# One logits product of 42 columns per token tile, denominators summed by GpSimd, and batch 0's lane on three shared banks

## The chip, the core and the metric

The kernel runs on one core of a Trainium2 chip. The metric is the device time of one execution in microseconds (us), as the median of several runs. The engines are TensorE (PE in the profile, its weight loads PEld), VectorE (DVE), ScalarE (ACT), GpSimd (POOL) and SyncE (SP), which issues most of the DMAs.

## The reference

Two parts are chained. The first is an attention through 49 "agents" for four batches of 10048 tokens of 128 channels; the second sends each token to one expert of 16 (4 groups of 4), a two-layer network.

```python
a2k = softmax(scale * agents @ k.T)      # 49 x 10048 for each batch
agent_v = a2k @ v                        # 49 x 128
x = softmax(scale * q @ agents.T) @ agent_v   # 10048 x 128 for each batch
g = argmax(x @ w_group)                  # 4 groups
e = argmax(x @ w_expert[g])              # 4 experts of the group
out = p_g * p_e * (relu(x @ w1[g, e]) @ w2[g, e])
```

All inputs and outputs are float32.

## The kernel before, in words

**Tiles.** The tokens of a batch are 79 tiles of 128 (the last has 64). A chunk is 8 tiles; there are ten a batch. The attention's output x is never made for the tokens: each token keeps its 49 numerators (as a high and a low float16 part, 98 rows, transposed into a tile `et`), and the agents' values are multiplied into the expert's first matrix and into the routers' matrix. So the logits of a tile are the product of 98 rows of `et` with a small matrix `rh` of 98 x 2 x 21: 4 group logits, 16 expert logits and the numerators' sum, in a high and a low part.

**The main path.** Most tokens of a batch go to one expert, its "main" one. For each group of four tiles (`natural`, 20 a batch) the two functions `first` and `second` (lines 834 and 850) run eight units each: `first` multiplies `et` by a block of the expert's first matrix into a PSUM bank `ph` (128 x 512), ScalarE takes the ReLU as float16 (`hh`) and VectorE the remainder (`hl`); `second` comes eight units later and adds three products for each of four tiles into a bank `po`. After eight units VectorE scales `po` by the token's weight (`oo`) and SP writes it out. `ph` has three banks (pool `ps1`), `po` two (`ps2`); the other three banks (`psa`, tiles named `at`) are for everything else. Tokens of batch 0 that go to another expert are gathered and done with the last tiles of batch 3.

**Lanes.** Everything else of a batch is a lane: a Python generator that issues a few instructions and yields. Lane "a" is a batch's agents (`agents_of`, line 398): the keys' scores in `key_scores`, the maximum, and then the values. Lane "q" (`rest`, line 822) is its queries, its logits, its routing and its expert's weights. Lane "f" is batch 0's own queries, logits and routing from the second chunk on, and lane "o" prepares the left-over tokens of batch 0. A planner (`advance`, line 1144) interleaves lanes with the main path's units: each lane has a span of main path time (`SPAN_A`, `SPAN_Q`, `SPAN_F`, `SPAN_O`), the counted work of its instructions (VectorE's with weight 1, PE's and ScalarE's with 0.3), and an expected total in `WORK` (line 76); after each unit it is advanced to the part of its total that its span says. GpSimd's instructions are not counted. The first batch's start, before any main path, is written out by hand (`front`).

A lane's stages run skewed by one chunk each: for one step of the lane, the later stages of earlier chunks are issued first. For the queries the stages are the load, the split into high and low halves (ScalarE `xh`, GpSimd `xl`), the scores into a bank, the exponentials (VectorE takes the maximum `mq` and the difference `ef` out of that bank), the split of the numerators (`rows`), the transposes (two banks) and, in batch 0, the logits (one bank).

**Banks.** A lane takes its banks with `bank(b)` (line 148). For batches 1 to 3 it is always one of the three `at` banks. For batch 0 it goes round in eights:

```python
if b == 0:
    turns[0] += 1
    k = turns[0] % 8
    if k in (0, 3, 6):
        return ps1.tile([P, TS], F32, name="ph")
    if k in (1, 4):
        return ps2.tile([P, TQ, C], F32, name="po").rearrange("p a c -> p (a c)")
return psa.tile([P, 512], F32, name="at", tag="at")
```

**Logits** (`logits_of`, line 594). For each tile two matmuls of 21 columns, with the high and the low half of `rh`, add up in the same PSUM columns; ScalarE copies a chunk's 8 x 21 columns into `lg`.

**The agents' values** (`value_split`, line 352, and `value_products`, line 377; batches 1 to 3). VectorE subtracts the maximum from a chunk's scores in `S`, ScalarE takes the exponential and its float16 copy `sh`, GpSimd the remainder `sl` in pieces of three tiles (line 373). PE adds three products per tile (`vh` by `sh`, `vh` by `sl`, `vl` by `sh`) into 49 columns of one bank, `acc`, which is held for the whole stage. The denominators are summed on PE too: a matrix of ones times `sh` and times `sl`, four tiles (196 columns) at a time, into the next columns of the same bank.

The instructions that go through the counting helper carry its line, L122, in the profile; GpSimd's carry their own.

Of the kernel before, what the change touches and what calls it, by code (L numbers as in the profile page):

```python
# [10 lines left out]
F32 = mybir.dt.float32  # L11
F16 = mybir.dt.float16
I32 = mybir.dt.int32
AF = mybir.ActivationFunctionType
ALU = mybir.AluOpType
AX = mybir.AxisListType
# [4 lines left out]
P = 128  # L21
# [3 lines left out]
NA = 49  # L25
# [4 lines left out]
NT = 79  # L30
NTP = NT + 1
LAST = N - (NT - 1) * P
CT = 8
TS = 512
TQ = TS // P
# [6 lines left out]
RW = NA + 1  # L42
VS = 16.0
ES = 2.0 ** 14
ZT = 4
IC = 8
GT = 16
NGR = -(-NT // GT)
# [24 lines left out]
SPAN_O = (2.93, 3.32)  # L73
SPAN_F = (0.0, 0.52)
WA = (0.3, 1.0, 0.3)
WORK = {"a": 38e3, "q": 42e3, "o": 37.5e3, "f": 38e3}


def const_pack():
# [47 lines left out]
def build(ctx, tc, qT, kT, v, agT, wr, w1, w2, cpk, out):  # L127
    nc = tc.nc
    pool, sync = nc.gpsimd, nc.sync
    work = np.zeros(3)  # L130
    pe = Counted(nc.tensor, work, 0, 4.0, 0.42)
    vec = Counted(nc.vector, work, 1, 65.0, 1.04)
    act = Counted(nc.scalar, work, 2, 100.0, 0.83)
# [4 lines left out]
    sm = ctx.enter_context(tc.tile_pool(name="sm", bufs=2))  # L138
# [4 lines left out]
    psa = ctx.enter_context(tc.tile_pool(name="psa", bufs=3, space=PSUM))  # L143

    turns = [0]
    loaded = {}

    def bank(b=1):

        if b == 0:  # L150
            turns[0] += 1
            k = turns[0] % 8
            if k in (0, 3, 6):
# [4 lines that stand above are left out]
# [21 lines left out]
    ones16 = const.tile([P, P], F16, name="ones16")  # L179
    vec.memset(ones16, 1.0)  # L180
    ones = const.tile([P, P], F32, name="ones")
# [52 lines left out]
    def skewed(n, *stages):  # L234

        for i in range(n + len(stages) - 1):
            yield "chunk"
            for k in reversed(range(len(stages))):
                if 0 <= i - k < n:
                    yield from stages[k](i - k)  # L240
# [8 lines left out]
    def key_load(b, ci, early=None):  # L249

        st = state[b]
        if ci == 0:
            st["S"] = rt.tile([P, NT, NA], F32, name="S", tag="S")
            st["mch"] = sm.tile([P, len(chunks), NA], F32, name="mch")
            st["part"] = []
        st["k", ci] = split_load("k", b, ci, early)
        yield

    def load_only(kind, b, ci):

        if (kind, b, ci) not in loaded:
            loaded[kind, b, ci] = load(kind, b, ci)
        yield
# [88 lines left out]
    def value_split(b, ci):  # L352

        st = state[b]
        S, mb = st["S"], st["part"][0][2]
        t0, t1 = chunks[ci]
        vf = st.pop(("v", ci))
        sh, sl = [mo.tile([P, CT, NA], F16, name=name) for name in ("sh", "sl")]
        vh, vl = [wk.tile([P, CT * P], F16, name=name, tag="x" + name[1]).rearrange("p (t c) -> p t c", c=C) for name in ("vh", "vl")]
        for a, z, m in ((t0, min(t1, NT - 1), P), (NT - 1, t1, LAST)):  # L360
            if z <= a:
                continue
            x, y = S[0:m, a:z], slice(a - t0, z - t0)
            vec.tensor_sub(out=x, in0=x, in1=mb[0:m].broadcast_to([m, z - a, NA]))
            act.activation(x, x, AF.Exp, bias=shift[0:m])
            act.activation(vh[0:m, y], vf[0:m, y], AF.Copy, scale=VS)
            yield
            act.activation(sh[0:m, y], x, AF.Copy)
            vec.scalar_tensor_tensor(out=vl[0:m, y], in0=vf[0:m, y], scalar=VS, in1=vh[0:m, y], op0=ALU.mult, op1=ALU.subtract)
            for i in range(0, z - a, 3):  # L370
                j = slice(i, min(i + 3, z - a))
                w = slice(y.start + j.start, y.start + j.stop)
                pool.tensor_sub(out=sl[0:m, w], in0=x[:, j], in1=sh[0:m, w])  # L373
            yield
        st["v", ci] = sh, sl, vh, vl

    def value_products(b, ci):

        st = state[b]
        sh, sl, vh, vl = st.pop(("v", ci))  # L380
        if ci == 0:
            st["acc"] = bank(1)
        acc = st["acc"]
        t0, t1 = chunks[ci]
        for t in range(t0, t1):
            m = min(P, N - t * P)
            i = t - t0
            for x, y in (vh, sh), (vh, sl), (vl, sh):
                pe.matmul(acc[:, 0:NA], x[0:m, i], y[0:m, i], start=(t == 0 and x is vh and y is sh), stop=False)
            if i % 4 == 3 or t == NT - 1:  # L390
                yield
        for a, z, m in [(t, min(t + ZT, t1, NT - 1), P) for t in range(t0, min(t1, NT - 1), ZT)] + [(NT - 1, NT, LAST)] * (t1 == NT):
            o = acc[:, NA + (a % ZT) * NA:NA + (a % ZT + z - a) * NA]
            for y in sh, sl:
                pe.matmul(o, ones16[0:m], y[0:m, a - t0:z - t0].rearrange("p t a -> p (t a)"), start=False, stop=(z == NT and y is sl))
        yield

    def agents_of(b):

        state[b] = {}  # L400
        st = state[b]
        n = len(chunks)
        yield from skewed(n, lambda ci: load_only("k", b, ci), lambda ci: key_load(b, ci), lambda ci: key_scores(b, ci))
        yield from key_max(b, 0, n, False)
        yield from skewed(n, lambda ci: value_load(b, ci), lambda ci: value_split(b, ci), lambda ci: value_products(b, ci))
        yield
        acc = st["acc"]
        za = sm.tile([P, NA], F32, name="za2")
        vec.tensor_reduce(out=za, in_=acc[:, NA:(ZT + 1) * NA].rearrange("p (t a) -> p a t", a=NA), axis=AX.X, op=ALU.add)
        vec.tensor_scalar(out=za, in0=za, scalar1=1e-9 * ES, scalar2=None, op0=ALU.add)  # L410
        vec.reciprocal(out=za, in_=za)
        avT = sm.tile([P, NA], F32, name="avT")
        vec.scalar_tensor_tensor(out=avT, in0=acc[:, 0:NA], scalar=1.0 / VS, in1=za, op0=ALU.mult, op1=ALU.mult)
        yield
        yield from agents_scaled(b, avT)
# [106 lines left out]
    def queries_of(b, early=None, cs=None, *more):  # L522

        cs = list(range(len(chunks))) if cs is None else cs
        xs = [{} for _ in chunks]
        stages = [query_load, query_scores, query_exp, query_split, query_turn]
        if early:
            groups = [stages[:2]] + [[x] for x in stages[2:]]
        else:
            groups = [[lambda b, ci, x, early: load_only("q", b, ci)]] + [stages[:1], stages[1:2], stages[2:4], stages[4:]]  # L530

        def run(group):
            def f(i):
                for stage in group:
                    yield from stage(b, cs[i], xs[cs[i]], early)
            return f

        yield from skewed(len(cs), *[run(g) for g in groups], *[lambda i, f=f: f(b, cs[i]) for f in more])
# [53 lines left out]
    NL = NG + NE + 1  # L592

    def logits_of(b, ci):

        st = state[b]
        if ci == 0:
            st["lg"] = rt.tile([P, NL, NTP], F32, name="lg", tag="lg")
            vec.memset(st["lg"][:, :, NT:NTP], 1.0)
        lg = st["lg"]  # L600
        t0, t1 = chunks[ci]
        pl = bank(b)
        for t in range(t0, t1):
            o = pl[:, (t - t0) * NL:(t - t0 + 1) * NL]
            for h in range(2):
                pe.matmul(o, st["et", t // TQ][:, t % TQ * P:(t % TQ + 1) * P], st["rh"][:, h], start=(h == 0), stop=(h == 1))
            if t % 4 == 3:
                yield
        plv = pl[:, 0:(t1 - t0) * NL].rearrange("p (t g) -> p t g", g=NL)
        act.activation(lg[:, :, t0:t1].rearrange("p g t -> p t g"), plv, AF.Copy)  # L610
        yield

    def routing(b, t0, t1):
# [253 lines left out]
    def natural(b, w):  # L867

        t, n = TILES[w]
        return dict(b=b, w=w, t=t, n=n, per=1, units=FB, et=state[b]["et", w],  # L870
                    wb=wbuf[b % 2].bitcast(F16), done=rows_out)
# [280 lines left out]
    def lane(kind, b, gen, span):  # L1152
        lanes.append(dict(kind=kind, b=b, gen=gen, start=span[0], end=span[1], total=WORK[kind], done=0.0))

    later = queries_of(0, None, list(range(1, len(chunks))), logits_of, ranged)
    for _ in range(AHEAD):
        for x in later:
# [6 lines left out]
    for b in range(1, B):  # L1164
        lane("a", b, agents_of(b), SPAN_A[b])
        lane("q", b, rest(b), SPAN_Q[b])
# [3 lines left out]
    for b in range(B):  # L1170
# [3 lines left out]
        for w in range(NW):  # L1174
            y = next(y for y in lanes if y["kind"] == "f")
            while b == 0 and (("et", w) not in state[0] or state[0]["covered"] < TILES[w][0]):
                advance(y, y["done"] / y["total"] + 1e-6)
            x = natural(b, w)
            units = [(x, k) for k in range(FB)]
            if b == B - 1 and w >= NW - TAKEN:  # L1180
                j = w - (NW - TAKEN)
# [4 lines left out]
                y = late.pop(j)  # L1186
# [49 lines left out]
```

## Time and profile before

| | |
|---|---|
| median of three runs | 1016.2 us (1013.15 to 1016.98) |
| the profiled execution's own time | 1020.15 us |
| its span, first to last instruction | 1018.4 us |
| mean granted clock of PE | 0.974 |
| busy: PE, PEld, DVE, ACT, POOL | 946.3, 763.3, 781.8, 653.9, 331.7 us |

The profile has names of tiles on both sides of an arrow: `hl<-ph,hh` writes `hl` from `ph` and `hh`. A duration of a matmul runs from its start to the end of its results; matmuls overlap, so what one costs in a stream is the time from start to start. In the timeline, the bracket at the end of a row is the idle time ahead of it and what ended it. In a row of a group, after the bar come the busy time, the mean of one in ns, and the idle time ahead with what ended it. Pieces of a timeline that are merged have a count (x2) and one duration for all.

### The profile page before, as it was taken

The page shows a single profiled execution, that of the slowest core. Times are in us where ns is not written, and L with a number is a line of the kernel's source. Part 1 is how long each engine was busy: PE and PEld are TensorE (multiplying, and loading weights), DVE is VectorE, ACT ScalarE, POOL GpSimd, SP SyncE. Part 2 cuts the span into 40 slices and gives each one's busy share as a digit, 9 for nine tenths or more (in the row PEclk, how much of TensorE's full clock was granted, in tenths as well). Part 3 has the DMA queues.
Part 4 walks back from the last instruction along what each step waited for, and adds up shares of the span by engine and source line. Part 5 has one row for each costly group of instructions (what it writes and reads, how often), then busy time and mean ns, then how long its engine had stood idle before and what let it go on. Part 6 is the DMA issues. An engine that isn't in the chain of part 4 may idle for free. (4 is left out here: it accounts for less than half of the span.)

```text
span 1018.4 us, 32113 instructions
## 1 busy us (share of the span) xinstructions
PE 946.3 (93%) x13645; PEld 763.3 (75%) x13645; DVE 781.8 (77%) x1508; ACT 653.9 (64%) x1168; POOL 331.7 (33%) x548
## 2 busy tenths in 40 slices
PE   4968998989997999999989999999999999999996
PEld 3846777777876878888768778887777778888885
DVE  5668889977697896786977877877989966666663
ACT  4436577688745876977467778876555555555552
POOL 2334237278303624850025327630000021322211
PEclk9968999989998999999999999999999999999999
DMA  9634235444036633410463434311233062333330
GB/s 296 208 115 150 60 105 185 126 137 122 23 106 236 195 102 106 122 40 23 131 222 111 143 95 126 98 29 40 75 113 111 23 205 66 119 117 110 90 108 26
DMA packets 107451, 117.45 MB, mean 115 GB/s; under 512 B 5479, under 2 KB 92648, under 8 KB 105120
## 3 DMA queue, kind: packets, MB, share of 16 engines
q1 hardware_dynamic: 105760, 113.40, 35.8%
q0 software_dynamic: 1536, 1.90, 0.8%
q8 instruction: 108, 1.77, 0.7%
q14 instruction: 47, 0.39, 0.1%
HBM read 81.92 MB, written 33.65 MB: 113 GB/s over the span
## 5 line engine op out<-in xcount | busy, mean ns | idle before, releaser
L122 DVE SCALAR_TENSOR_TENSOR hl<-ph,hh 128x512 f16<-128x512 f32 (+1 forms) x688 | 458.7, 678 | 145.2 <-ACT hh L122 143.9
L122 PEld LDWEIGHTS <-hh 128*128 128x128 f16 x5440 | 448.1, 98 | 148.1 <-issue 4.2
L122 ACT ACTIVATE hh<-ph 128x512 f16<-128x512 f32 (+1 forms) x688 | 402.2, 591 | 220.7 <-PE ph L122 208.0
L122 PE MATMUL po<-wbuf,hh 128*128 128x128 f16 x5440 | 537.9, 220 | 0.0
L122 PE MATMUL po<-wbuf,hl 128*128 128x128 f16 x2720 | 496.0, 220 | 0.0
L122 PE MATMUL ph<-et,wbuf 98*128 98x512 f16 (+1 forms) x1280 | 384.0, 380 | 23.4 <-DVE hl L122 21.2
L122 PEld LDWEIGHTS <-hl 128*128 128x128 f16 x2720 | 266.8, 98 | 2.4 <-issue 0.6
L231 POOL TENSOR_TENSOR xl<-xf,xh 128x256 f16<-128x256 f32 (+1 forms) x288 | 189.4, 690 | 238.6 <-ACT xh L122 229.6
L122 PEld LDWEIGHTS <-wbuf 98*128 98x128 f16 x1472 | 116.8, 98 | 38.1 <-issue 30.5
L122 ACT ACTIVATE xh<-xf 128x1024 f16<-128x1024 f32 x80 | 83.3, 1041 | 53.2 <-PE at L122 27.7
L373 POOL TENSOR_TENSOR sl<-S,sh 128x147 f16<-128x147 f32 (+1 forms) x90 | 43.4, 510 | 97.0 <-ACT sh L122 93.8
L122 PEld LDWEIGHTS <-xh 128*128 128x128 f16 x1264 | 60.6, 99 | 14.6 <-ACT xh L122 12.7
L1065 POOL DMA_INDIRECT out<-oo,sidx x24 | 24.1, 1004 | 138.6 <-DVE oo L122 135.0
L1043 POOL DMA_INDIRECT er<-erow,gidx x24 | 24.7, 1030 | 134.7 <-DVE gidx L122 127.7
L574 POOL TENSOR_TENSOR rows<-ef,rows 128x147 f16<-128x147 f32 (+2 forms) x117 | 50.8, 461 | 52.3 <-ACT rows L122 52.3
L122 PEld LDWEIGHTS <-xl 128*128 128x128 f16 x632 | 53.0, 99 | 12.4 <-POOL xl L231 9.2
L122 PE MATMUL at<-agh,xl 128*128 128x49 f16 x538 | 54.1, 186 | 6.6 <-POOL xl L231 6.6
L122 DVE TENSOR_TENSOR oo<-po,cw 128x512 f32<-128x512 f32 x80 | 53.8, 673 | 6.0 <-PE po L122 5.7
L122 PE MATMUL at<-agh,xh 128*128 128x49 f16 x538 | 54.4, 187 | 3.0 <-ACT xh L122 3.0
L122 PE MATMUL at<-agl,xh 128*128 128x49 f16 x538 | 54.2, 186 | 0.0
L122 ACT ACTIVATE et<-at 98x512 f16<-98x512 f16 x68 | 39.4, 590 | 7.1 <-PE at L122 7.0
L122 DVE SCALAR_TENSOR_TENSOR vl<-vf,vh 128x1024 f16<-128x1024 f32 (+2 forms) x33 | 38.7, 1172 | 5.6 <-ACT vh L122 5.5
(278 smaller groups left out, 873.3 us busy)
## 6 DMA issues: line engine op xcount, KB each, us to landing
out<-oo SPq DMA_DIRECT2D x76, 256.0 KB, 2.7
xf<-kT SPq DMA_DIRECT2D x36, 512.0 KB, 4.1
vf<-v SPq DMA_DIRECT2D x36, 512.0 KB, 5.7
xf<-qT SPq DMA_DIRECT2D x36, 512.0 KB, 4.1
wbuf<-wall SPq DMA_DIRECT2D x12, 1024.0 KB, 4.9
erow<-rows SPq DMA_DIRECT2D x3, 1975.0 KB, 7.3
w1f<-w SPq DMA_DIRECT2D x6, 512.0 KB, 4.0
w2f<-w SPq DMA_DIRECT2D x6, 512.0 KB, 7.2
```

Source lines behind the costliest of these rows:

```text
L122: return f(*a, **k)
L231: pool.tensor_sub(out=xl[:, y], in0=xf[:, y], in1=xh[:, y])
L373: pool.tensor_sub(out=sl[0:m, w], in0=x[:, j], in1=sh[0:m, w])
L574: (vec if early else pool).tensor_sub(out=rows[:, w, NA:2 * NA], in0=ef[:, y], in1=rows[:, w, 0:NA])
L1043: pool.indirect_dma_start(out=er[:, q], out_offset=None, in_=erow[b][:, :], in_offset=bass.IndirectOffsetOnAxis(ap=place(b, j * GW + q)[0] ...
L1065: ins = pool.indirect_dma_start(out=out, out_offset=bass.IndirectOffsetOnAxis(ap=place(x["b"], x["j"] * GW + q)[1], axis=0), in_=o[:, q], ...
```

## The change

Four edits:

- **Logits.** One matmul of 42 columns per tile (both halves of `rh` side by side) takes the place of the two of 21. VectorE then adds the two halves while it moves a chunk from PSUM into `lg`; ScalarE's copy goes.
- **The agents' denominators.** The matmuls against ones in `value_products` go. GpSimd instead adds each piece of `S` into a tile `zs` of 8 x 49 columns (the first chunk is copied), right behind the subtraction for `sl`. After the last chunk one float32 matmul of 392 columns sums `zs` over the partitions, and VectorE's sum over tiles reads its bank.
- **Banks.** A flag `alone` is set while batch 0's start runs and cleared ahead of the lane "f"; from there batch 0 also uses the three `at` banks only. Lane "o" of batch 0 is affected in the same way.
- **Totals.** The expected totals of the lanes "a", "q" and "f" follow the new counts.

```diff
-WORK = {"a": 38e3, "q": 42e3, "o": 37.5e3, "f": 38e3}
+WORK = {"a": 37e3, "q": 44.6e3, "o": 37.5e3, "f": 40.8e3}
...
+    alone = [True]
...
-        if b == 0:
+        if alone[0] and b == 0:
...
+        if ci == 0:
+            st["zs"] = sm.tile([P, CT, NA], F32, name="zs", bufs=1)
...
                 pool.tensor_sub(out=sl[0:m, w], in0=x[:, j], in1=sh[0:m, w])
+                if t0 == 0:
+                    pool.tensor_copy(out=st["zs"][0:m, w], in_=x[:, j])
+                else:
+                    pool.tensor_add(out=st["zs"][0:m, w], in0=st["zs"][0:m, w], in1=x[:, j])
...
-        for a, z, m in [(t, min(t + ZT, t1, NT - 1), P) for t in range(t0, min(t1, NT - 1), ZT)] + [(NT - 1, NT, LAST)] * (t1 == NT):
-            o = acc[:, NA + (a % ZT) * NA:NA + (a % ZT + z - a) * NA]
-            for y in sh, sl:
-                pe.matmul(o, ones16[0:m], y[0:m, a - t0:z - t0].rearrange("p t a -> p (t a)"), start=False, stop=(z == NT and y is sl))
...
+        zp = bank(1)[:, 0:CT * NA]
+        pe.matmul(zp, ones, st["zs"].rearrange("p t a -> p (t a)"), start=True, stop=True)
+        yield
...
-        vec.tensor_reduce(out=za, in_=acc[:, NA:(ZT + 1) * NA].rearrange("p (t a) -> p a t", a=NA), axis=AX.X, op=ALU.add)
+        vec.tensor_reduce(out=za, in_=zp.rearrange("p (t a) -> p a t", a=NA), axis=AX.X, op=ALU.add)
...
-            o = pl[:, (t - t0) * NL:(t - t0 + 1) * NL]
-            for h in range(2):
-                pe.matmul(o, st["et", t // TQ][:, t % TQ * P:(t % TQ + 1) * P], st["rh"][:, h], start=(h == 0), stop=(h == 1))
+            o = pl[:, (t - t0) * 2 * NL:(t - t0 + 1) * 2 * NL]
+            pe.matmul(o, st["et", t // TQ][:, t % TQ * P:(t % TQ + 1) * P], st["rh"].rearrange("p h g -> p (h g)"), start=True, stop=True)
...
-        plv = pl[:, 0:(t1 - t0) * NL].rearrange("p (t g) -> p t g", g=NL)
-        act.activation(lg[:, :, t0:t1].rearrange("p g t -> p t g"), plv, AF.Copy)
+        plv = pl[:, 0:(t1 - t0) * 2 * NL].rearrange("p (t h g) -> p t g h", h=2, g=NL)
+        vec.tensor_reduce(out=lg[:, :, t0:t1].rearrange("p g t -> p t g"), in_=plv, axis=AX.X, op=ALU.add)
...
+    alone[0] = False
     later = queries_of(0, None, list(range(1, len(chunks))), logits_of, ranged)
```

More of the change, by code (lines that the diff above doesn't have):

```diff
@@ L44 @@
 ES = 2.0 ** 14
-ZT = 4
 IC = 8
@@ L388, in value_products @@
             for x, y in (vh, sh), (vh, sl), (vl, sh):
-                pe.matmul(acc[:, 0:NA], x[0:m, i], y[0:m, i], start=(t == 0 and x is vh and y is sh), stop=False)
+                pe.matmul(acc[:, 0:NA], x[0:m, i], y[0:m, i], start=(t == 0 and x is vh and y is sh), stop=(t == NT - 1 and x is vl))
             if i % 4 == 3 or t == NT - 1:
                 yield
-        for a, z, m in [(t, min(t + ZT, t1, NT - 1), P) for t in range(t0, min(t1, NT - 1), ZT)] + [(NT - 1, NT, LAST)] * (t1 == NT):
-            o = acc[:, NA + (a % ZT) * NA:NA + (a % ZT + z - a) * NA]
-            for y in sh, sl:
-                pe.matmul(o, ones16[0:m], y[0:m, a - t0:z - t0].rearrange("p t a -> p (t a)"), start=False, stop=(z == NT and y is sl))
         yield
```

## The prediction

> **What bounds the kernel now.** I read the page first: how busy each engine is, TensorE (PE) in 40 slices, and the chain that ended last.
>
> ```profile
> span 1018.4 us, 32113 instructions
> ...
> PE 946.3 (93%) x13645; PEld 763.3 (75%) x13645; DVE 781.8 (77%) x1508; ACT 653.9 (64%) x1168; POOL 331.7 (33%) x548
> ...
> PE   4968998989997999999989999999999999999996
> ...
> PE 30%; DVE 6%; ACT 1%; DMA 1%; issue 0%; POOL 0%; SPq 0%; ACTq 0%
> ```
>
> PE is busy nearly everywhere, and the pieces of the chain that were followed lie on PE. But an average hides stages, so next the stretches of the four batches, cut where the main work passes from one to the next (columns: stretch, length, then busy us and instructions of PE, PEld, DVE, ACT, POOL, granted clock, DMA share, GB/s):
>
> ```profile
> 76.00:204.00 128.00, 115.72 (x1744) 90.98 (x1745) 113.50 (x255) 88.73 (x166) 53.59 (x94) 0.96 0.42 126
> 204.00:306.00 102.00, 95.31 (x1529) 77.28 (x1529) 77.48 (x152) 74.98 (x139) 49.80 (x88) 0.97 0.32 98
> 306.00:510.00 204.00, 195.00 (x2995) 157.54 (x2995) 162.10 (x290) 148.25 (x267) 79.61 (x140) 0.98 0.40 120
> 510.00:714.00 204.00, 199.66 (x3067) 161.09 (x3067) 160.14 (x267) 149.83 (x270) 78.28 (x140) 0.99 0.36 108
> ```
>
> From 204 to 714 PE is busy 490 of 510 us: what leaves PE there shortens the run nearly one for one. From 76 to 204, batch 0 with its own lane, PE (115.7) and VectorE (113.5 of 128) are about equally full, and a gap comes from whichever is late. Batch 0 is therefore the doubtful part.
>
> **Logits on PE.** Now two matmuls of 21 columns per token tile; afterwards one of 42.
>
> ```profile
> L122 PE MATMUL at<-rh,et x520: 172/172/186, 60.0 to 694.8; 98*128 98x21 f16 x174
> L122 PE MATMUL po<-rh,et x64: 172/172/202, 64.4 to 176.2; 98*128 98x21 f16 x64
> L122 PE MATMUL ph<-rh,et x48: 172/172/178, 84.2 to 147.4; 98*128 98x21 f16 x48
> ```
>
> That is 632 = 2 x 316. The 172 ns are one matmul from end to end; what a stream pays is the step from start to start:
>
> ```profile
> 688.86 1.55 PE L122 MATMUL at<-rh,et 98*128 98x21 f16 x56
> ```
>
> (1.55 - 0.17) / 55 = 25.1 ns. For 42 columns the nearest row is the scores' 49, first and last of 20:
>
> ```profile
> 89.51 0.19 PE L122 MATMUL ph<-agh,xh 128*128 128x49 f16 x1
> ...
> 89.99 0.18 PE L122 MATMUL ph<-agl,xh 128*128 128x49 f16 x1
> ```
>
> 0.48 / 19 = 25.3 ns, so the step doesn't depend on columns in this range and 316 steps go: 8.0 us. Were the cost by column instead, nothing would go; 25.3 is taken, as 49 lies above 42. 237 of the 316 tiles are in batches 1 to 3 (6.0 us, in stretches where PE is full), 79 in batch 0 (2.0 us).
>
> **The agents' denominators on PE.** Per batch 38 matmuls of 196 columns, two of 98 and two of 49 against ones go:
>
> ```profile
> 389.84 0.25 PE L122 MATMUL at<-sh,ones 128*128 128x196 f16 x1
> ...
> 390.09 0.25 PE L122 MATMUL at<-sl,ones 128*128 128x196 f16 x1
> 390.18 0.60 PE L122 MATMUL ph<-et,wbuf 98*128 98x512 f16 x2
> ...
> 391.28 0.60 PE L122 MATMUL ph<-et,wbuf 98*128 98x512 f16 x2
> ```
>
> Four take 0.34 us, 85 ns each: 38 x 0.085 + 0.14 = 3.37 us a batch, 10.1 in all. Added is one f32 matmul of 392 columns a batch; the nearest is the weights' f32 one of 512 (two records are one product):
>
> ```profile
> 812.17 1.08 PE L122 MATMUL at<-w1f,at 128*128 128x512 f32 x2
> 813.08 0.60 PE L122 MATMUL ph<-et,wbuf 98*128 98x512 f16 x2
> ```
>
> 0.91 us, by columns 0.70, three times 2.1. Net 8.0 us off PE. It waits for GpSimd's last sum; behind it on PE stand the main matmuls. I cost that wait at nothing, because a whole chunk step of the lane lies between: without that cover it is up to one chunk's sums, 1.5 us a batch (the subtractions' price below).
>
> So in the stretches where PE is full 14.0 us go: 4.7 in 204 to 306, 9.3 in 306 to 714.
>
> **Logits from ScalarE to VectorE.** 40 copies leave ScalarE, and 40 sums of 336 elements arrive on VectorE.
>
> ```profile
> L122 DVE TENSOR_REDUCE mch<-S 128x49 f32<-128x392 f32 x36 | 29.9, 834 | 12.9 <-ACT S L122 12.8
> ...
> L122 DVE TENSOR_REDUCE mq<-at 128x8 f32<-128x392 f32 x32 | 17.9, 560 | 5.9 <-PE at L122 5.7
> ...
> L122 ACT ACTIVATE lg<-at 128x168 f32<-128x168 f32 x29 | 12.2, 456 | 4.0 <-PE at L122 4.0
> ...
> L122 DVE TENSOR_REDUCE za<-at 128x49 f32<-128x196 f32 x3 | 1.1, 357 | 0.0
> ```
>
> The two reads of PSUM, 392 elements in 560 ns and 196 in 357, give 1.04 ns an element and 0.15 fixed: 0.50 us here. The read of SBUF scaled, 336/392 x 834 = 0.72, is the upper bound. In batches 1 to 3 VectorE has the room (160 of 204 us), so the 5 us each cost nothing; without that cover they would cost 15. In batch 0 nine of them, 4.5 us, fall where VectorE is nearly full: between 0 and 4.5 (6.5 by the upper price), I take half, 2.3, and set nothing against it for the 2.0 us that PE saves there. The sum also makes VectorE wait for the products as ScalarE did (4.0 us in the last ACT row); behind it queue the hl subtractions for which the ph ring waits. The first chunk's logits stand ahead of the main work; there 0.50 takes the place of 0.46 and PE's eight steps less make that good.
>
> **GpSimd's sums.** 90 additions more, one beside each subtraction:
>
> ```profile
> L373 POOL TENSOR_TENSOR sl<-S,sh 128x147 f16<-128x147 f32 (+1 forms) x90 | 43.4, 510 | 97.0 <-ACT sh L122 93.8
> ```
>
> At that price 14.5 us a batch, 43.4 in all; the first chunk's copies, with one input, come to no more. Where a values stage and a query lane overlap:
>
> ```profile
> 216.00:252.00 36.00, 34.39 (x604) 28.77 (x602) 27.07 (x41) 31.95 (x58) 29.87 (x52) 0.97 0.49 144
> 402.00:444.00 42.00, 41.84 (x715) 34.99 (x713) 33.28 (x59) 35.95 (x66) 31.46 (x55) 1.00 0.45 131
> 612.00:660.00 48.00, 47.46 (x800) 39.49 (x798) 37.68 (x62) 40.24 (x72) 35.16 (x62) 1.00 0.41 118
> ```
>
> POOL has 6 us free in the first, 10 and 13 in the others; four or five of the ten chunks' additions bring 6 to 7. So it fills up in batch 1's, and low halves (xl, sl) come late to PE: I halve the 4.7 us of that stretch (between 0 and all of it) and leave the other two whole.
>
> **Batch 0's banks.** Before, its lane takes banks of the main path's rings:
>
> ```profile
> 96.01 1.01 PE L122 MATMUL ph<-et,wbuf 98*128 98x512 f16 x2 [2.87 <-DVE hl L122]
> ...
> 126.90 0.60 PE L122 MATMUL ph<-et,wbuf 98*128 98x512 f16 x2 [1.67 <-DVE ef L122]
> ```
>
> ```profile
> 94.12 0.55 DVE L122 TENSOR_REDUCE mq<-ph 128x8 f32<-128x392 f32 x1
> ...
> 96.58 0.55 DVE L122 TENSOR_TENSOR ef<-ph,mq 128x392 f32<-128x392 f32 x1
> ```
>
> The scores written from 89.51 lie in a ph bank until 97.1, so PE could run only two units ahead; at 126.9 PE waits for such a tile outright. Both gaps are at most 4.5 us. A third bank is worth one unit, from the ph at 390.18 to the next at 391.28 in the listing above, 1.1 us, so I take 2 x 1.1 = 2.2 off. The bounds are 0 and 4.5, and a loss is below (rival 3).
>
> The new lane totals only spread the same steps; I cost them at nothing, covered by work that other lanes always have ready, and at up to 1 us a batch if one is drained late.
>
> **Sum.** -9.3 - 2.35 + 2.3 - 2.2 = -11.5 us. The profiled execution took 1020.15 us (span 1018.4), so 1008.6; it lies 0.4% over the median 1016.2 of the three runs, which scales to 1004.7. About 0.5%, 5.1 us, is what a measurement of this kernel can tell from no change: faster is below 1011.1, slower above 1021.3.
>
> **Rivals.**
>
> 1. *Batch 0 gains more.* After the 2.87 us gap the clock drops:
>
> ```profile
> 92.00:96.00 4.00, 1.14 (x18) 0.99 (x17) 4.00 (x9) 0.74 (x2) 2.15 (x4) 0.90 0.21 28
> 96.00:100.00 4.00, 3.99 (x24) 2.72 (x24) 3.01 (x10) 2.17 (x5) 0.24 (x1) 0.50 0.48 171
> 100.00:104.00 4.00, 4.00 (x40) 3.08 (x39) 2.93 (x9) 1.54 (x3) 0.94 (x3) 0.75 0.00 0
> ```
>
> 4 x 0.5 + 4 x 0.25 = 3.0 us of PE's work lost. A gap that is shorter by a unit may not trip it, and the full 4.5 us of gaps may go: 1004.7 - 3.0 - 2.3 = 999. Against it: VectorE is busy all of 92 to 96. The Trainium skill ("TensorE: Matmul & The Clock Gate", Part 1) says that half clock follows an idle window of about 3.4 us; by that neither gap would trip it and this rival would give 1002; the trace shows 0.50 after 2.87 us, and I go by the trace.
>
> 2. *GpSimd's additions hold VectorE up.* A subtraction of 64 elements beside GpSimd's xl, and one without:
>
> ```profile
> 91.66 0.69 DVE L122 TENSOR_TENSOR rd<-lg,gm 128x64 f32<-128x64 f32 x1
> ...
> 123.10 0.22 DVE L122 TENSOR_TENSOR rd<-lg,gm 128x64 f32<-128x64 f32 x1
> ```
>
> 0.47 us is the price of one collision. If each of the some 13 chunks' additions (39) in the three stretches costs VectorE that, 18 us arrive where it has 8.9, 8.7 and 10.3 us free. It decides where the delay falls just ahead of an hl that the ring waits for; for half of them that is 9 us: 1014, within 0.5%. The Trainium skill ("SBUF — State Buffer", Who interferes with whom) says so as a rule: a VectorE instruction with two SBUF inputs and a GpSimd instruction that reads SBUF exclude each other for the whole instruction. By that rule the rows above agree.
>
> 3. *The three shared banks starve batch 0's lane: slower.* A scores tile is held 7.6 us (89.5 to 97.1), so two banks are left for the logits, the two turns and the keys of batch 1, and one once its accumulator is taken near 186. Each take that finds none stops PE in its queue, and all main matmuls behind it. With 27 takes (three for each of nine chunks) at 1 us, and the 2.2 us not won, it is 1004.7 + 27 + 2.2 = 1034. It beats the gain from about 0.5 us a take on. Against it: batches 1 to 3 run queries and values on these three banks with PE busy 96% of the time.
>
> 4. *42 columns cost twice 21:* the 6.0 us stay, 1010.7. The row of 49 columns speaks against it.
>
> **How the numbers follow.** The forecast, with its own range 998 to 1010 (batch 0's half counted whole or not at all, the clock kept or not), has 0.58; rival 1 0.14, rival 2 0.15, rival 3 0.08, rival 4 0.05. Faster: 0.58 + 0.14, the lower part of rival 2 (0.04) and half of rival 4 (0.02): 0.78. Slower is rival 3, 0.08; the rest, 0.14, is the same. The range goes from rival 1 with some more of batch 0's gaps, 993, to rival 2 with a late start of a lane, 1017; rival 3 and the tails stay out.
>
> **What would show it.** In the changed profile: 316 matmuls rh,et at 25 ns a step; none against ones with 196 columns; PE's busy time down by some 14 to 16 us; a VectorE sum for lg of 0.50 us; POOL up by 43 us, close to full in batch 1's values stage. In batch 0's stretch no scores tile lies in ph, and the 1.67 us wait for ef is gone. I am wrong if PE waits for at banks (ef, et, lg as releasers) add up to over 5 us between 76 and 204, if waits for xl and sl grow by more than 5 us, or if PE's busy time falls as said and the span doesn't.

## The result, and the profile after

The changed kernel takes 1027.75 us (median of six runs, 1023.4 to 1028.95); the kernel before, beside it on the same chip, 1017.19 us (six runs, 1013.15 to 1020.87). The ratio is 1.010 with a 95% interval of 1.0071 to 1.0128: it is slower by 1%, where 1004.7 us and faster were forecast. The profiled execution took 1026.81 us.

The page of the changed kernel: span, busy time, and TensorE in 40 slices.

```profile
span 1024.7 us, 31347 instructions
...
PE 940.1 (92%) x13209; PEld 750.8 (73%) x13209; DVE 802.7 (78%) x1548; ACT 640.5 (63%) x1128; POOL 376.4 (37%) x638
...
PE   3969988868998989999999999999999999999997
```

436 matmuls are gone, but PE is busy for only 6.2 us less, and idle for 84.6 us where it was 72.1. The slices (25.6 us each) have a 6 from 205 to 230 us, where batch 0's main work runs beside batch 1's values; before there was an 8. The four stretches of the prediction, after:

```profile
76.00:204.00 128.00, 117.02 (x1740) 91.96 (x1738) 116.67 (x271) 89.01 (x161) 59.16 (x108) 0.96 0.42 128
204.00:306.00 102.00, 87.58 (x1315) 69.24 (x1314) 77.97 (x147) 68.20 (x125) 55.08 (x105) 0.95 0.26 78
306.00:510.00 204.00, 193.62 (x2872) 153.39 (x2869) 167.81 (x288) 143.15 (x254) 95.19 (x170) 0.97 0.39 117
510.00:714.00 204.00, 194.92 (x2914) 154.92 (x2912) 161.65 (x281) 145.04 (x257) 96.02 (x170) 0.98 0.38 116
```

The operations themselves came out as forecast. The tile `rh`, then the groups of `lg` and `zs`:

```profile
L121 PE MATMUL at<-rh,et x316: 180/180/207, 59.7 to 706.9; 98*128 98x42 f16 x158
```

```profile
L379 POOL TENSOR_TENSOR zs<-zs,S 128x147 f32<-128x147 f32 (+2 forms) x81 | 43.4, 567 | 8.5 <-ACT S L121 8.5
...
L121 DVE TENSOR_REDUCE lg<-at 128x168 f32<-128x336 f32 (+1 forms) x40 | 19.6, 496 | 1.3 <-PE at L121 1.1
```

What changed is who makes PE wait (the chain of waits, summed: us, times, longest), first before, then after:

```profile
PE ph L122 <- DVE hl L122: 21.2, 23, 3.9
...
PE at L122 <- POOL xl L231: 6.6, 22, 0.9
...
PE at L122 <- DVE ef L122: 1.9, 2, 1.5
...
PE at L122 <- POOL rows L574: 0.7, 1, 0.7
```

```profile
PE ph L121 <- DVE hl L121: 21.3, 26, 2.5
PE at L121 <- POOL xl L231: 12.7, 26, 3.3
PE po L121 <- ACT xh L121: 9.5, 2, 8.0
PE at L121 <- DVE ef L121: 5.9, 5, 3.5
PE at L121 <- POOL rows L579: 5.5, 4, 2.8
```

The waits for GpSimd's `xl` and `rows` and for `ef` grew by some 15 us. Those for `hl`, which the prediction feared, stayed in total but not in place: up to the end of batch 0 they fell from 12.2 to 7.3 us, and over batches 1 and 2 they rose by 4.6 us. The same row for batches 1 and 2 alone, before and after:

```profile
PE ph L122 <- DVE hl L122: 9.0, 12, 3.0
```

```profile
PE ph L121 <- DVE hl L121: 13.6, 18, 2.1
```

**Where the time is lost.** The main path makes 20 groups of four tiles a batch, each ending in an `oo`; the starts of the same `oo` in two traces show which stretch got longer. Batch 1, from the last `oo` of batch 0 to its own, before and after:

```profile
345.58 0.56 DVE L122 TENSOR_TENSOR oo<-po,cw 128x384 f32<-128x384 f32 x1
...
562.69 0.55 DVE L122 TENSOR_TENSOR oo<-po,cw 128x384 f32<-128x384 f32 x1
```

```profile
346.05 0.54 DVE L121 TENSOR_TENSOR oo<-po,cw 128x384 f32<-128x384 f32 x1
...
567.08 0.55 DVE L121 TENSOR_TENSOR oo<-po,cw 128x384 f32<-128x384 f32 x1
```

217.1 us became 221.0. The table does this for every kernel of this study. "0b" is batch 0 from its 9th group to its last, where batch 1's values run; "xl" is PE's total wait for `xl` in batches 1 and 2. Ratios are of several runs each against the kernel before on the same chip; the stretches are of the one profiled execution.

| kernel | agents' total / counted | ratio (95%) | 0b | batch 1 | batch 2 | xl |
|---|---|---|---|---|---|---|
| before | 38 / 37.6 | 1 | 144.3 | 217.1 | 215.0 | 0.5, 0.5 |
| after | 37 / 36.9 | 1.010 (1.0071 to 1.0128) | 150.9 | 221.0 | 218.8 | 1.8, 2.0 |
| logits_only | 38 / 37.6 | 0.9913 (0.989 to 0.9936) | 137.4 | 215.7 | 214.9 | 0.5, 0.5 |
| banks_only | 38 / 37.6 | 0.999 (0.9971 to 1.001) | 142.6 | 217.1 | 215.3 | 0.5, 0.5 |
| sums_only | 37 / 36.9 | 1.0133 (1.0093 to 1.0173) | 148.1 | 221.1 | 219.5 | 2.2, 2.3 |
| logits_banks | 38 / 37.6 | 0.9905 (0.9878 to 0.9933) | 137.3 | 214.5 | 215.4 | 0.5, 0.5 |
| logits_sums | 37 / 36.9 | 1.0043 (1.0025 to 1.006) | 144.7 | 219.9 | 218.5 | 2.0, 2.0 |
| no_sum | 37 / 36.9 | 0.994 (0.9919 to 0.9962) | 139.9 | 219.1 | 217.8 | 2.0, 2.0 |
| write_only | 37 / 36.9 | 0.9991 (0.9969 to 1.0013) | 144.3 | 218.0 | 217.8 | 2.0, 2.0 |
| late_sums | 37 / 36.9 | 1.0084 (1.0053 to 1.0115) | 152.3 | 221.0 | 218.4 | 1.9, 2.0 |
| vec_sums | 41.7 / 41.7 | 1.0001 (0.9977 to 1.0025) | 147.0 | 215.5 | 214.5 | 0, 0 |
| no_sum_old_plan | 38 / 37.6 | 0.9884 (0.9844 to 0.9925) | 139.6 | 214.9 | 214.1 | 0.6, 0.6 |
| after_old_plan | 38 / 37.6 | 0.998 (0.996 to 0.9999) | 145.2 | 217.2 | 216.0 | 0.6, 0.6 |
| vec_sums_old_plan | 38 / 37.6 | 1.0001 (0.9981 to 1.0021) | 151.7 | 215.3 | 214.7 | 0.6, 0.6 |
| after_a38 | 38 / 36.9 | 0.9989 (0.9972 to 1.0007) | 148.4 | 216.7 | 214.0 | 0, 0 |
| after_a374 | 37.4 / 36.9 | 1.004 (1.0015 to 1.0066) | 148.4 | 216.2 | 215.3 | 0.6, 0.6 |
| before_a376 | 37.6 / 37.6 | 1.007 (1.0043 to 1.0098) | 140.7 | 220.5 | 217.7 | 2.1, 2.1 |
| logits_banks_a376 | 37.6 / 37.6 | 0.9958 (0.9939 to 0.9976) | 139.8 | 218.9 | 218.8 | 2.1, 2.1 |
| after_a39 | 39 / 36.9 | 1.0023 (1.0 to 1.0046) | 146.7 | 216.7 | 221.5 | 1.1, 1.1 |
| logits_banks_a39 | 39 / 37.6 | 0.989 (0.9866 to 0.9913) | 139.4 | 213.0 | 214.2 | 0, 0 |

Totals and counts are in thousands. One caution: the profiled execution of the kernel before lies 4 us above its median, so differences of about 4 us in all between two traces are no finding; the ratios are. The stretch after batch 2 is left out: it takes some 232 us in most traces and some 241 in those of the six kernels beside which the kernel before, too, took 8 to 10 us more. So the stretches of a row do not add up to its ratio.

### The profile page after: what moved, and what is told of

It is laid out like the page before. It is cut to its first block, busy times and chain, and to the rows that moved or that the text cites. A ratio compares the mean times of both kernels' runs of the same rounds, so it can differ in the third digit from the quotient of the medians.

```text
span 1024.7 us, 31347 instructions
## 1 busy us (share of the span) xinstructions
PE 940.1 (92%) x13209; PEld 750.8 (73%) x13209; DVE 802.7 (78%) x1548; ACT 640.5 (63%) x1128; POOL 376.4 (37%) x638
## 3 DMA queue, kind: packets, MB, share of 16 engines
q8 instruction: 105, 1.72, 0.7%
## 5 line engine op out<-in xcount | busy, mean ns | idle before, releaser
L121 PE MATMUL at<-agh,xl 128*128 128x49 f16 x577 | 59.5, 189 | 13.1 <-POOL xl L231 12.7
L121 PE MATMUL at<-agh,xh 128*128 128x49 f16 x577 | 60.1, 189 | 2.4 <-ACT xh L121 2.2
L121 PE MATMUL at<-agl,xh 128*128 128x49 f16 x577 | 59.7, 188 | 0.0
L121 ACT ACTIVATE et<-at 98x512 f16<-98x512 f16 x74 | 42.6, 589 | 14.9 <-PE at L121 14.7
L121 DVE SCALAR_TENSOR_TENSOR vl<-vf,vh 128x1024 f16<-128x1024 f32 (+2 forms) x33 | 43.3, 1313 | 9.9 <-ACT vh L121 8.6
L379 POOL TENSOR_TENSOR zs<-zs,S 128x147 f32<-128x147 f32 (+2 forms) x81 | 43.4, 567 | 8.5 <-ACT S L121 8.5
```

What stands on the lines that cost most here:

```text
L121: return f(*a, **k)
L379: pool.tensor_add(out=st["zs"][0:m, w], in0=st["zs"][0:m, w], in1=x[:, j])
```

## Experiments: the parts alone

The first question was which of the edits costs. Four kernels make one edit or two, a fifth leaves out the banks.

**logits_only**: the kernel before with the product of 42 columns, VectorE's sum and the totals of lanes "q" and "f".

```diff
-WORK = {"a": 38e3, "q": 42e3, "o": 37.5e3, "f": 38e3}
+WORK = {"a": 38e3, "q": 44.6e3, "o": 37.5e3, "f": 40.8e3}
...
+            pe.matmul(o, st["et", t // TQ][:, t % TQ * P:(t % TQ + 1) * P], st["rh"].rearrange("p h g -> p (h g)"), start=True, stop=True)
...
+        vec.tensor_reduce(out=lg[:, :, t0:t1].rearrange("p g t -> p t g"), in_=plv, axis=AX.X, op=ALU.add)
```

> The kernel before with the product of 42 columns and VectorE's sum alone (totals of the query lanes 44.6e3 and 40.8e3). Theory S: 6 us off PE in batches 1 to 3 show, 1009 to 1013 us. Rival B: the same. Rival L: no gain or a loss, 1017 to 1025.

Measured 0.9913: some 9 us won. In its trace nearly all of it lies in batch 0; batches 1 and 2 are only 1.5 us shorter together. No run separates the product from the new totals of "q" and "f".

**sums_only**: the kernel before with GpSimd's sums and the agents' total of 37 thousand.

```diff
+WORK = {"a": 37e3, "q": 42e3, "o": 37.5e3, "f": 38e3}
...
+                    pool.tensor_add(out=st["zs"][0:m, w], in0=st["zs"][0:m, w], in1=x[:, j])
```

> The kernel before with GpSimd's sums alone (total of the agents' lane 37e3). Theory S: GpSimd's additions cause the loss, in batch 0 from tile 8 on (about +11 us) and in batches 1 and 2 (about +6 each): 1017 + 23 = about 1038 us. Rival B (the three shared banks make PE wait late in batch 0): the sums take 8 us off PE, about 1009 to 1012. Rival L (the logits' sum on VectorE and the new totals cost): the same 1009 to 1012.

Measured 1.0133. Alone, this edit with its total loses as much as the whole change.

**banks_only**: the flag `alone` and nothing else.

```diff
-        if b == 0:
+        if alone[0] and b == 0:
```

> The kernel before with the banks of batch 0's lane alone. Theory S: the 6 us that batch 0's first nine tiles gained are kept, about 1011 us. Rival B: they are lost again by the end of batch 0, where the third bank is the values' accumulator: 1017 to 1025. Rival L: about 1011.

Measured 0.999, no change that can be told.

**logits_banks**: the change without the sums and without the agents' total.

```diff
-WORK = {"a": 37e3, "q": 44.6e3, "o": 37.5e3, "f": 40.8e3}
+WORK = {"a": 38e3, "q": 44.6e3, "o": 37.5e3, "f": 40.8e3}
...
-                    pool.tensor_add(out=st["zs"][0:m, w], in0=st["zs"][0:m, w], in1=x[:, j])
...
+                pe.matmul(o, ones16[0:m], y[0:m, a - t0:z - t0].rearrange("p t a -> p (t a)"), start=False, stop=(z == NT and y is sl))
```

> The change without GpSimd's sums (denominators on PE as before). Theory S: gains of both, about 1003 to 1007 us. Rival B: 1012 to 1020. Rival L: 1012 to 1020.

Measured 0.9905, which can't be told from the logits alone.

**logits_sums**: the change without the flag `alone`.

```diff
-        if alone[0] and b == 0:
+        if b == 0:
```

> The change without its banks part. The sums cost 14 us alone and 19 in the whole change. If the three shared banks make the sums dearer (rival 3 in a small form: a held scores tile, the accumulator and one free bank), this is 3 to 6 us above before; if not, it is as the change, 8 to 12 us above before.

Measured 1.0043. With the sums in, the banks cost some 6 us (1.010 against 1.0043), all of it in 0b (150.9 against 144.7); without them they cost nothing. In the traces of 0b PE's waits for `ef` are 3.5 us with the shared banks and 0.5 without, and the granted clock is 0.955 against 0.976. Why this happens only with the sums stays open.

## Experiments: what in the sums costs

**no_sum**: the change without the additions; `zs` keeps the first chunk, so the denominators hold one chunk of ten.

```diff
-                else:
-                    pool.tensor_add(out=st["zs"][0:m, w], in0=st["zs"][0:m, w], in1=x[:, j])
```

> The change with GpSimd's additions left out (only the first chunk's copy is kept, so the denominators hold one chunk of ten). It shows what taking the ones matmuls off PE is worth where nothing takes their place. Theories P (shared port) and Q (GpSimd's queue): the 9 us below before of the logits and banks, and up to 8 more: 9 to 17 us below before. Rival V (PE is no longer the bound there): not better than 9 us below before.

Measured 0.994. This was the surprise: with no addition at all, and the ones matmuls gone, it is no faster than `logits_banks` (0.9905), which still has those matmuls; its ratio is even higher, though the two intervals just overlap. This pointed to a cost other than GpSimd's work.

**write_only**: as many GpSimd instructions, each writing 392 columns of zeros into a part of `S` that is used up, one step of the lane later.

```diff
+                    pool.memset(st["S"][0:m, t0:min(t1, NT - 1)], 0.0) if z < NT else pool.memset(st["S"][0:m, a:z], 0.0)
```

> The change with GpSimd's additions after the first chunk replaced by as many memsets of 392 columns, one lane step later, into the part of S that has been used up: GpSimd is as busy but reads no SBUF in them (the denominators again hold one chunk of ten). Theory P (an addition that reads SBUF locks VectorE's two-input instructions out, and hl comes late): within 3 us of the kernel without sums. Theory Q (GpSimd's queue is full, so xl, sl and rows come late to PE): within 5 us of the change, 5 to 10 us above before.

**late_sums**: the additions in that same place.

```diff
+                    pool.tensor_add(out=st["zs"][0:m, w], in0=st["zs"][0:m, w], in1=st["S"][0:m, s])
```

> The change with GpSimd's additions issued one lane step later, with the chunk's products, so that they no longer stand ahead of the chunk's own sl. Theory Q: half of the loss comes back, 0 to 5 us above before. Theory P: as many collisions, as the change, 8 to 12 us above before.

Measured 0.9991 and 1.0084. Beside `no_sum`, instructions that only write cost 5 us and the additions 15. The groups of `write_only`, then of `late_sums`:

```profile
L121 DVE SCALAR_TENSOR_TENSOR vl<-vf,vh 128x1024 f16<-128x1024 f32 (+2 forms) x33 | 38.7, 1177 | 9.5 <-ACT vh L121 8.1 <-PE ph L121 1.3
...
L393 POOL MEMSET S<- 128x392 f32 (+2 forms) x81 | 32.9, 408 | 4.1
```

```profile
L393 POOL TENSOR_TENSOR zs<-zs,S 128x147 f32<-128x147 f32 (+2 forms) x81 | 43.7, 571 | 8.5 <-ACT S L121 8.5
...
L121 DVE SCALAR_TENSOR_TENSOR vl<-vf,vh 128x1024 f16<-128x1024 f32 (+2 forms) x33 | 42.3, 1286 | 10.8 <-ACT vh L121 9.4 <-PE ph L121 1.3
```

VectorE's `vl`, which has two inputs in SBUF, has a mean of 1286 ns beside additions and 1177 beside writes. The Trainium skill ("SBUF — State Buffer", Who interferes with whom) states that such an instruction excludes a GpSimd instruction that reads SBUF, not one that only writes it; the means lie that way. But most of their difference is one `vl` of 4.19 us in `late_sums`; the median of the 128x1024 ones is 1.23 us in both, so these rows are weak evidence. An addition also holds GpSimd 0.16 us longer (571 against 408 ns), 13 us over 81, so how much of the 9.5 us between the two is reading and how much is length stays open. A step's delay (`late_sums` against the change) doesn't help.

How one collision grows can be read in the changed kernel. VectorE, then GpSimd, then PE:

```profile
243.67 4.17 DVE L121 SCALAR_TENSOR_TENSOR vl<-vf,vh 128x1024 f16<-128x1024 f32 x1
247.76 0.55 DVE L121 TENSOR_TENSOR ef<-at,mq 128x392 f32<-128x392 f32 x1
```

```profile
243.96 0.29 POOL L379 TENSOR_TENSOR zs<-zs,S 64x49 f32<-64x49 f32 x1
244.21 2.54 POOL L231 TENSOR_TENSOR xl<-xf,xh 128x256 f16<-128x256 f32 x4
```

```profile
248.37 0.42 PE L121 MATMUL at<-ident,rows 128*98 128x128 f16 x4 [3.54 <-DVE ef L121]
```

`vl` takes 4.17 us, where the median of its shape is 1.23: it ends about one `vl` after GpSimd's row of instructions does. Behind it on VectorE is `ef`, and PE stands idle for 3.54 us. The four transposes do not read this `ef` (its exponential is taken only later, at 249.32 us); they wait for the `at` bank that it reads out. So this is a wait for a shared bank, of the kind that rival 3 named. It is the only `vl` of this trace above 2 us. The other form is plain queueing, where the additions are ahead of the next chunk's halves:

```profile
202.99 4.30 POOL L379 TENSOR_TENSOR zs<-zs,S 128x147 f32<-128x147 f32 x6 [1.23 <-ACT S L121]
207.25 2.54 POOL L231 TENSOR_TENSOR xl<-xf,xh 128x256 f16<-128x256 f32 x4
```

```profile
207.97 0.20 PE L121 MATMUL at<-agh,xl 128*128 128x49 f16 x1 [3.28 <-POOL xl L231]
```

Six additions take 4.30 us instead of the 3.1 that six subtractions take by the prediction's row, `xl` starts after them, and PE waits 3.28 us in the middle of a chunk's scores. The clock then falls (windows of 4 us, granted clock third from the end):

```profile
204.00:208.00 4.00, 0.59 (x7) 0.20 (x6) 3.11 (x6) 1.69 (x4) 4.00 (x7) 1.00 0.01 4
208.00:212.00 4.00, 3.42 (x36) 2.43 (x37) 1.64 (x3) 1.48 (x2) 3.50 (x7) 0.53 0.31 38
212.00:216.00 4.00, 4.00 (x66) 3.61 (x64) 2.52 (x5) 3.12 (x6) 4.00 (x9) 0.61 1.00 352
```

A gap of 3.28 us costs up to another 4 x 0.47 + 4 x 0.39 = 3.4 us by the lower clock. Over 204 to 306 GpSimd is busy 55 of 102 us: what stands ahead of `xl` in its queue, not its load, does this. In `no_sum`, under the same plan, the longest wait at this spot is 1.37 us.

**vec_sums**: VectorE sums, one addition for each chunk; 41.7 thousand for the agents.

```diff
-                    pool.tensor_add(out=st["zs"][0:m, w], in0=st["zs"][0:m, w], in1=x[:, j])
...
+                vec.tensor_add(out=st["zs"][0:m, y], in0=st["zs"][0:m, y], in1=x)
```

> The change with the sums on VectorE, one instruction of 392 columns a chunk (30 of about 0.56 us), lane total 41.7e3. Theories P and Q: GpSimd is as before, VectorE has 40 us of room a batch in batches 1 and 2, so 9 to 14 us below before. Rival V: VectorE becomes the bound, 0 to 5 us below before.

Measured 1.0001. The loss against `logits_banks` (10 us) now lies in 0b alone (147.0 against 137.3); batches 1 and 2 take about what they take there. In 0b PE waits as long for the first `xl` as in the change, though GpSimd adds nothing; here three subtractions for `sl` stand ahead of it:

```profile
205.56 2.76 POOL L375 TENSOR_TENSOR sl<-S,sh 128x147 f16<-128x147 f32 x3 [11.86 <-ACT sh L121]
```

```profile
209.00 0.20 PE L121 MATMUL at<-agh,xl 128*128 128x49 f16 x1 [3.20 <-POOL xl L231]
```

So a wait of that length needs no additions; here another block of GpSimd's instructions ahead of `xl` gave it. How much of the additions' cost goes this way is not shown.

## Experiments: the plan

In the traces `no_sum` takes 4.6 and 2.4 us more than `logits_banks` in batches 1 and 2, and in each of them PE's wait for `xl`, at one spot where the next batch's query lane begins, is 2.0 us instead of 0.5. So the counted work came under suspicion.

**no_sum_old_plan**, **after_old_plan**, **vec_sums_old_plan**: the planner sees the counts of before. The steps add the ones matmuls' count though none is issued, the new instructions are not counted, the total is 38 thousand, and the added yield is gone.

```diff
+WORK = {"a": 38e3, "q": 44.6e3, "o": 37.5e3, "f": 40.8e3}
...
+            work[0] += 2 * (4.0 + 0.42 * (z - a) * NA)
...
-        pe.matmul(zp, ones, st["zs"].rearrange("p t a -> p (t a)"), start=True, stop=True)
-        yield
+        nc.tensor.matmul(zp, ones, st["zs"].rearrange("p t a -> p (t a)"), start=True, stop=True)
```

> The kernel without GpSimd's additions (denominators hold one chunk of ten) with the planner's counts kept as if the ones matmuls were still there (agents' total 38e3), so that the lanes' steps are handed out between the main units as in the version with logits and banks alone, which was 9 us below before. Theory N (the new counts move the lane's steps and eat what PE saves): 12 to 17 us below before. Theory V (where PE is shortened it waits for xl, ef and hl instead): 5 to 10 us below, as without the old counts.

> The change with the same old counts. Theory N: 5 us or more below the change, 0 to 5 us above before. Theory V with P (collisions of additions that read SBUF): as the change, 8 to 12 us above before.

> The sums on VectorE (one addition of 392 columns a chunk) with the old counts. Theory N: 8 to 12 us below before. Theory V: within 4 us of before.

Measured 0.9884, 0.998 and 1.0001. The same instructions under the old plan gain 5.7 us without additions and 12 us with GpSimd's. Under it the additions themselves cost 0.998 - 0.9884, some 10 us, and VectorE's cost no less (12).

Which part of the plan? Four kernels alter one number, the agents' total.

```diff
+WORK = {"a": 38e3, "q": 44.6e3, "o": 37.5e3, "f": 40.8e3}
```

**after_a38** (the change with 38 thousand), **after_a374** (with 37.4):

> The changed kernel with one number of the plan altered: the agents' total is 38 thousand as before, not 37. The steps count 36.9 thousand in all, so each lane a now runs 2.9 % ahead of its span instead of 0.2 %. Theory T (the lead that the total gives is what the plan's change costs): the ratio to before falls from 1.010 to about that of the changed kernel under all the old counts, 0.998; between 0.995 and 1.003. Theory C (the counts of the single steps and the added yield cost it, which make the agents' products come in two pieces just ahead of the query lane's first scores): it stays at 1.007 to 1.013.

> The changed kernel with an agents' total of 37.4 thousand: a lead of 1.3 %, the one that the kernel before has (37.55 thousand counted of 38). Theory T: 0.997 to 1.003. Theory C: 1.007 to 1.013. If the time is ragged in such totals, with no rule in it, this run and the one with 38 thousand differ by more than 0.5 %.

**before_a376** and **logits_banks_a376**: no sums, 37.6 in place of 38.

> The kernel before with an agents' total of 37.6 thousand in place of 38, so that its lanes a lead by 0.1 % as in the changed kernel; nothing else. Theory T: it loses what the plan's change cost the changed kernel, 1.004 to 1.012. Theory C: 0.998 to 1.002.

> The change without the GpSimd sums (0.9905 with a total of 38 thousand), with an agents' total of 37.6 thousand. Theory T: 0.995 to 1.003. Theory C: 0.988 to 0.993.

Measured 0.9989, 1.004, 1.007 and 0.9958. (The profiled execution of `after_a374` lies 4 us under its median, so its row of the table flatters it.) One number gives back 11 us of the change, all that the old plan gave, and takes 7 us from the kernel before, in which nothing else was touched. The counts and the yield are therefore not needed to explain what the plan costs. Both kernels with 37.6 lose in batches 1 and 2, at the same spot. There, in `before_a376` (ScalarE, GpSimd, PE):

```profile
393.80 1.06 ACT L122 ACTIVATE xh<-xf 128x1024 f16<-128x1024 f32 x1 [0.35 <-PE at L122]
394.94 3.37 POOL L231 TENSOR_TENSOR xl<-xf,xh 128x256 f16<-128x256 f32 x4 [5.47 <-ACT xh L122]
...
395.07 0.19 PE L122 MATMUL at<-agh,xh 128*128 128x49 f16 x1
...
396.49 0.20 PE L122 MATMUL at<-agh,xl 128*128 128x49 f16 x1 [1.20 <-POOL xl L231]
...
397.11 0.20 PE L122 MATMUL at<-agh,xl 128*128 128x49 f16 x1 [0.31 <-POOL xl L231]
```

And in the kernel before:

```profile
396.49 1.06 ACT L122 ACTIVATE xh<-xf 128x1024 f16<-128x1024 f32 x1 [0.66 <-PE at L122]
397.62 2.55 POOL L231 TENSOR_TENSOR xl<-xf,xh 128x256 f16<-128x256 f32 x4 [5.45 <-ACT xh L122]
...
398.87 0.19 PE L122 MATMUL at<-agh,xh 128*128 128x49 f16 x1
...
398.92 0.18 PE L122 MATMUL at<-agh,xl 128*128 128x49 f16 x1
```

From the start of `xh` to the first score are 2.38 us before and 1.27 us with 37.6: one unit of the main path (1.1 us in the prediction's listing) now stands between them instead of two. GpSimd needs that unit for the first `xl`. Without it PE is in the scores with nothing else to do, waits 1.20 us and then 0.31 for each further piece, and the clock follows:

```profile
396.00:400.00 4.00, 2.60 (x34) 1.93 (x35) 1.64 (x3) 1.21 (x2) 3.57 (x8) 0.85 0.37 72
400.00:404.00 4.00, 4.00 (x38) 2.97 (x37) 1.79 (x3) 2.45 (x5) 3.41 (x7) 0.73 0.89 254
```

4 x 0.15 + 4 x 0.27 = 1.7 us more, nearly 4 in all. In the kernel before, the clock stays at 1.00 there. In the changed kernel PE waits 1.13 us at 402 us, and then 0.31, 0.20 and 0.20. With 38 thousand (`after_a38`) these waits are gone, and batches 1 and 2 are 9.1 us shorter: PE is idle for 4.2 us less and busy, at a higher clock (0.977 to 0.984, 0.992 to 1.000), for 4.8 us less. The table's last column shows it across the study: the eight kernels that wait 1.8 to 2.3 us for `xl` take 217.7 to 221.1 us in batches 1 and 2; the others wait 0 to 1.1, and but for one stretch take 213.0 to 217.2.

**after_a39** and **logits_banks_a39**: is more lead better still?

```diff
+WORK = {"a": 39e3, "q": 44.6e3, "o": 37.5e3, "f": 40.8e3}
```

> The changed kernel with an agents' total of 39 thousand (36.9 counted): a lead of 5.6 %. With 37, 37.4 and 38 thousand it measured 1.010, 1.004 and 0.999. Theory L (the more lead, the better: the agents' last products stand further from the query lane's first scores): 0.990 to 0.998. Theory R (what counts is how the last steps of one lane fall between the first of the next, so that the time is ragged in the total): no further gain, 0.998 to 1.008.

> The change without the GpSimd sums, with an agents' total of 39 thousand (37.6 counted): a lead of 3.8 %. With 37.6 and 38 thousand it measured 0.996 and 0.9905. Theory L: 0.983 to 0.990, the best version so far. Theory R: 0.989 to 0.998.

Measured 1.0023 and 0.989. It is no rule of "more lead": with the sums 39 is no better than 38 (batch 2 takes 221.5 us in that profiled execution, which is 4.6 us above its own median), and `vec_sums` has no lead at all and a free start of the query lane. What counts, as far as these traces show, is how the two lanes' steps fall among the main path's units; a rule for it in the total was not found (1.010, 1.004, 0.999 and 1.002 for 37, 37.4, 38 and 39). `logits_banks` (0.9905), `logits_banks_a39` (0.989) and `logits_only` (0.9913) beat both kernels and can't be told apart.

## Why the prediction was wrong, by its own steps

Three of its steps failed. The lane totals, costed at nothing, cost 11 us and turned the sign. GpSimd's additions, put at 2.35 us, cost some 10. And PE's 8.0 us from the ones matmuls, counted nearly whole, brought some 2.

- **Logits: the prices right, the place wrong.** The step is 25.7 ns for 42 columns ((0.36 - 0.18) / 7 from a row of eight at 704 us), as assumed from the row of 49. VectorE's sum takes 0.50 us as worked out. Alone the edit brought 9 us, where its two terms, 6.0 off and 2.3 on, make 3.7. But of the 6.0 the prediction put 4.0 into batches 1 and 2, which are only 1.5 us shorter in the trace of `logits_only`; the 2.3 us that it feared in batch 0 do not show, and 0b is 7 us shorter. These are single traces, and the one of the kernel before lies 4 us over its median, but the gain came where it was not forecast: that this term was beaten was luck.
- **"What leaves PE shortens the run nearly one for one": failed.** This is the step behind most of the gain. The two rows below each are batches 1 and 2 from last `oo` to last `oo`, of `logits_banks` and of `no_sum_old_plan`, which differ in the ones matmuls and the little that stands for them (the first chunk's copies, one float32 matmul):

```profile
334.30:548.80 214.50, 209.36 (x3141) 167.73 (x3140) 175.31 (x311) 152.53 (x272) 78.64 (x141) 1.00 0.38 114
548.80:764.20 215.40, 208.07 (x3010) 165.87 (x3009) 182.40 (x338) 144.00 (x259) 57.62 (x109) 1.00 0.32 94
```

```profile
334.60:549.50 214.90, 206.87 (x3102) 164.67 (x3100) 175.62 (x310) 152.30 (x271) 78.53 (x144) 1.00 0.38 114
549.50:763.60 214.10, 205.55 (x2971) 162.72 (x2969) 182.32 (x337) 143.89 (x259) 58.03 (x112) 1.00 0.32 94
```

PE is busy for 5.0 us less and the time is shorter by 0.9; PE's idle time grows instead (the waits for `hl` from 8.8 to 10.0 us, for `ef` from 0.6 to 1.7, for `sl` from 0 to 1.3). By the ratios the same step is worth 2 us of 1016 (0.9905 to 0.9884, by their intervals between nothing and 7), where the prediction had 8.0. A PE that is busy 97% of a stretch still had waits set by other engines, and in these two traces the work taken out had been filling them.
- **GpSimd's additions at half of 4.7 us: mis-sized.** They cost some 10 us with a good plan (`after_old_plan` against `no_sum_old_plan`). In those two traces 5.6 us of it lie in 0b and 4.2 in batches 1 and 2, where the prediction set nothing. It reckoned with GpSimd filling up from 216 to 252 us. After the change GpSimd is as busy there as before, 29.9 of 36 us, but PE is busy for 27.8 us where it was 34.4:

```profile
216.00:252.00 36.00, 27.77 (x446) 21.78 (x444) 24.89 (x38) 28.19 (x53) 29.91 (x59) 0.96 0.44 130
```

The long waits in the changed kernel come from a block of additions ahead of `xl` (3.28 us) and from one `vl` behind GpSimd's row (3.54 us). Rival 2 had the second mechanism, at 9 us, and saw it end in `hl`. In batches 1 and 2 the waits for `hl` did grow; between `no_sum_old_plan` and `after_old_plan` it is from 10.0 to 12.3 us there. Which part of the 10 us goes which way was not separated.
- **Lane totals "at nothing", "up to 1 us a batch": failed, and decided the sign.** The total alone is worth 11 us on the changed kernel and 7 us on the one before. The assumed cover, "work that other lanes always have ready", does not exist inside one step: while a score waited 1.20 us for `xl` in `before_a376`, PE ran nothing of what stood behind it, and the next main matmul came after the scores' last piece.
- **Banks: the two gaps right, the gain not shown.** The 2.87 us gap at 96 us is gone (PE is busy all of 92 to 104 after, at a clock of 0.99), and so is the 1.67 us wait. Alone the edit measured 1 us, which can be told neither from nothing nor from the 2.2 that were forecast, and beside the sums it cost some 6. Rival 3 is out at its size and place: between 76 and 204 PE never waits for a bank released by `ef`, `et` or `lg`. But the 3.54 us at 248 us are such a wait. Rival 4 is out by the step of 25.7 ns.
- **The signs named beforehand did their work.** "Waits for xl and sl grow by more than 5 us" came true (6.6 to 12.7 for `xl`), and PE's busy time fell by 6.2 us, not 14 to 16, in large part because matmuls at a lower clock are longer: with the total of 38 the same 13209 matmuls take 933.6 us, 12.7 less than before (mean granted clock 0.975, against 0.970 in the changed kernel and 0.974 before).

Sum by ratios: logits 0.9913, banks -0.001, ones matmuls -0.002, additions +0.010, together 0.998 as `after_old_plan` measured; the total +0.011 to 0.012, together 1.010. Each term has an interval of some 0.002 to 0.005, so that they add up this closely is partly chance; and the sum leaves out that the banks cost more beside the sums.

## What to carry to other kernels

Before counting work that leaves the busiest engine as time won, ask what its remaining waits are: if other engines set them, the removed work was only filling. In a hand-scheduled kernel a constant of the planner is part of the change; try a few values of it on the old kernel too, since 1% in a total moved this one by 0.7%. In this kernel the place of a few cheap instructions in GpSimd's queue (PE waited 3.28 us for what stood behind them) mattered more than GpSimd's load (55 of 102 us).

## What was not expected of the hardware

- The clock falls after less than one long gap. Waits of 1.20 and three of 0.31 us within 2 us gave 0.85 and 0.73 over the next 8 us in `before_a376`. The changed kernel, after 1.13 us and three shorter ones, shows it in full:

```profile
404.00:408.00 4.00, 3.98 (x31) 3.15 (x32) 2.23 (x4) 2.56 (x4) 3.50 (x7) 0.50 0.75 216
```

The Trainium skill ("TensorE: Matmul & The Clock Gate", Part 1) gives, in its table of the two states, half clock after an idle window of about 3.4 us. By that row the gaps in `before_a376` would cost 2 us and not 4; the measured clock decides.
- A VectorE instruction with two inputs in SBUF can stand behind a whole row of GpSimd's: 4.17 us for a `vl` whose median is 1.23. It happened once in the changed kernel and once in `late_sums`; the longest `vl` of the kernel before is 1.72 us.
